# The last row tile's output in three pieces of 288, 160 and 128 columns instead of two of 288

## The chip, the cores and the metric

The kernel runs on one core of a Trainium2 chip. The time of a kernel is the device time of one execution in microseconds (us). The span of a profile is what the profiler saw of one execution; it is about 1.8 us shorter than the device time of the same run. Engines: PE is TensorE (PEld its weight loads), DVE VectorE, ACT ScalarE, SP SyncE, which here issues the stores. A semaphore is a counter that one unit raises and another waits for; a store raises its own in 16 steps, and the last step is called its landing. PSUM is the memory that matmuls write to. A drain is an instruction of an engine's queue; the first of SyncE's at the end of the program follows its waits for the stores.

## The reference

A two-layer block with squared ReLU, in bf16, on 2048 rows:

```
S, D, F = 2048, 576, 4608
h   = x @ w1 + b1            # [S, F]
h   = relu(h) ** 2
out = h @ w2 + b2            # [S, D]
```

## The kernel before

The rows are taken in four blocks of 512. For each block a first phase computes `hT` (36 tiles of 128 features), and a second one, `phase_b`, computes the output of four row tiles of 128 rows: 36 accumulated matmuls for each of two halves of 288 columns, one DVE add of the bias out of PSUM for each half, and a store. The very last row tile computes its halves one after the other, so that the first can be evacuated and stored while the second is computed:

```python
    def phase_b(sb, hT, last=False, dups=()):
        for jj in range(RT):
            ...
            po = [ps_o.tile([P, 512], FP32, name="po", tag="po") for _ in range(2)]
            o_sb = opool.tile([P, D], BF16, name="o_sb", tag="o_sb")
            # mmb(i, ft, h): matmul i of half h into po[h], 128 x 288
            # evac(h): o_sb half h = po[h] + b2_bc half h, on VectorE
            ...
            if last and jj == RT - 1:
                for h in range(2):
                    for i, ft in enumerate(ft_order):
                        mmb(i, ft, h)
                    evac(h)
                    keep(nc.sync.dma_start(out=out2[rt * P:(rt + 1) * P, h * DH:(h + 1) * DH], in_=o_sb[:, h * DH:(h + 1) * DH]))
                continue
            for i, ft in enumerate(ft_order):
                for h in range(2):
                    mmb(i, ft, h)
            for h in range(2):
                evac(h)
            keep(nc.sync.dma_start(out=out2[rt * P:(rt + 1) * P, :], in_=o_sb[:]))
```

After the kernel's last instruction, SyncE waits for the semaphores of everything still in flight; then the engines meet at two barriers and the program ends. The stores take turns on eight semaphores. The kernel's text shows none of this.

## Time and profile before

| | before |
|---|---|
| time, median of 3 runs (range) | 293.56 us (293.25 to 294.12) |
| span of the profile | 291.4 us |
| PE busy | 98% |
| last matmul starts | 287.42 us |
| last store issued, landed | 288.23, 289.80 us |

Lines from the page of the profile before: the busy time of each engine with its share of the span, then the shares of the chain that ended last.

```profile
span 291.4 us, 5457 instructions
PE 286.5 (98%) x2412; PEld 177.5 (61%) x2412; DVE 81.4 (28%) x189; ACT 93.7 (32%) x154; POOL 1.5 (1%) x8
...
PE 98%; ACT 0%; DVE 0%; issue 0%
```

PE is 98% busy and, after the loads at the start, has no idle time before its matmuls (0.0 in the groups of the page). Leaving the start aside, only two things can shorten this kernel: fewer PE cycles, or a shorter stretch after PE's last matmul. That stretch is seen in the timeline of the kernel before (start, length, engine, line, operation, count, and in brackets the idle time before it):

```profile
282.76 4.94 PE L233 MATMUL po<-w_sb,hT 128*128 128x288 bf16 x39
...
283.33 0.46 DVE L242 TENSOR_TENSOR o_sb<-po,b_bc 128x288 bf16<-128x288 f32 x1 [3.71 <-PE po L233]
283.82 4.74 SPq L254 DMA_DIRECT2D out_dram<-o_sb  x2
287.74 0.46 DVE L242 TENSOR_TENSOR o_sb<-po,b_bc 128x288 bf16<-128x288 f32 x1 [3.95 <-PE po L233]
```

The last add begins at 287.74 us and takes 0.46, and the second store follows at once. From there to the end of the span at 291.4 us there are no compute lines at all. SyncE's waits in this window (engine and line that waited, for whom, us in total, times, longest):

```profile
SPq L254 <- DVE o_sb L242: 7.7, 2, 4.0
SPq L317 <- DMA out_dram<-o_sb: 1.2, 1, 1.2
SPq L317 <- PEq L317: 0.6, 2, 0.5
```

The 1.2 us is the wait for the last store to land. L317 is the line that closes the program. The views merge what comes after it. The single records of SyncE in the trace show it (us; length in ns; the semaphores waited for):

```
288.227   332  store, increments 102
288.604    17  wait 103
288.664  1163  wait 104, 102      <- 102 lands at 289.80; the wait ends at 289.827
290.279    28  wait 106, 100      <- 452 ns after the wait before has ended
290.352    28  wait 107, 110
290.421    28  wait 108, 118
290.483    28  wait 109, 105
290.553    13  drain
```

The waits stand in a fixed order and follow each other at 60 to 73 ns when nothing blocks them. The prediction uses this order and pace in its step 4.

### The profile page before, as it was taken

The numbers are of one execution on the slowest core, as the hardware profiler recorded it, in microseconds if no ns is written. First come the engines' busy times: TensorE is split into PE (matmuls) and PEld (weight loads), VectorE is DVE, ScalarE is ACT, GpSimd is POOL, SyncE is SP. The second block draws the span as 40 slices with busy tenths as digits, with TensorE's granted clock in tenths as the row PEclk, the third lists the DMA queues.
The fourth block names the chain that finished last, engine by engine and source line by source line (L and its number), as shares of the span: only waits on it lengthen the run. The fifth ranks groups of instructions, "written<-read, shape, count | busy, mean of one in ns | idle before, by whom it ended". The sixth has DMA issues, their size and how long they took to land.

```text
span 291.4 us, 5457 instructions
## 1 busy us (share of the span) xinstructions
PE 286.5 (98%) x2412; PEld 177.5 (61%) x2412; DVE 81.4 (28%) x189; ACT 93.7 (32%) x154; POOL 1.5 (1%) x8
## 2 busy tenths in 40 slices
PE   8999999999999999999999999999999999999994
PEld 4444444444687875444477877444457878777783
DVE  3444544444531011544411110344440111110110
ACT  4666666666400001766620000466660000000000
POOL 2000000000000000000000000000000000000000
PEclk9999999999999999999999999999999999999999
DMA  6999999900000000000000000000000000000000
GB/s 183 201 200 175 233 358 326 158 7 2 0 23 0 23 20 20 2 1 2 2 0 20 23 3 20 20 2 0 2 0 2 20 24 20 23 0 23 20 23 21
DMA packets 27320, 16.05 MB, mean 55 GB/s; under 512 B 11284, under 2 KB 27296, under 8 KB 27296
## 3 DMA queue, kind: packets, MB, share of 16 engines
q1 hardware_dynamic: 26976, 15.39, 23.2%
q8 instruction: 19, 0.31, 0.4%
q10 hardware_dynamic: 288, 0.30, 0.3%
q14 instruction: 5, 0.04, 0.0%
q0 software_dynamic: 32, 0.01, 0.0%
HBM read 11.36 MB, written 2.36 MB: 47 GB/s over the span
## 4 chain that ended last, share of the span: by engine, by line
PE 98%; ACT 0%; DVE 0%; issue 0%
PE po L233 49%; PE ph L173 23%; PE ph L175 20%; PE pn L194 5%; PE wps L61 1%; PE pn L188 1%; ACT xTw L143 0%; ACT xTw L144 0%; DVE o_sb L242 0%; PE pn L190 0%; PE ta L138 0%; PE tb L141 0%; PE tb L142 0%; PE b1T_ps L151 0%
## 5 line engine op out<-in xcount | busy, mean ns | idle before, releaser
L233 PE MATMUL po<-w_sb,hT 128*128 128x288 bf16 x1152 | 141.6, 286 | 0.0
L233 PEld LDWEIGHTS <-hT 128*128 128x128 bf16 x1152 | 112.6, 98 | 29.3 <-issue 0.8
L175 PE MATMUL ph<-xTw,w_h 64*128 64x512 bf16 x576 | 125.0, 376 | 0.0
L173 PE MATMUL ph<-xTw,w_h 64*128 64x512 bf16 x576 | 125.0, 376 | 0.0
L161 ACT ACTIVATE r<-ph,b1T 128x512 bf16<-128x512 f32 x128 | 81.1, 685 | 41.0 <-PE ph L173 20.5
L162 DVE TENSOR_TENSOR hT<-r 128x512 bf16<-128x512 bf16 x144 | 61.2, 425 | 79.3 <-ACT r L161 79.3
L173 PEld LDWEIGHTS <-w_h 64*128 64x128 bf16 x576 | 54.0, 94 | 36.4
L175 PEld LDWEIGHTS <-w_h 64*128 64x128 bf16 x576 | 54.0, 94 | 32.3 <-DMA w_h<-in_w_dram 0.8
L242 DVE TENSOR_TENSOR o_sb<-po,b_bc 128x288 bf16<-128x288 f32 x32 | 13.2, 453 | 122.5 <-PE po L233 122.5
L161 ACT ACTIVATE r<-pn,b1T 128x512 bf16<-128x512 f32 x16 | 10.0, 688 | 80.9 <-PE pn L190 80.1
L194 PE MATMUL pn<-xTw,w1n 128*128 128x512 bf16 x64 | 14.5, 379 | 0.4 <-ACT xTw L144 0.4
L194 PEld LDWEIGHTS <-w1n 128*128 128x128 bf16 x64 | 6.1, 98 | 7.6 <-DMA w1n<-in_w_dram 0.6
L61 PE MATMUL wps<-const-bfloat16-1.0 128*128 128x512 bf16 (+1 forms) x7 | 2.9, 593 | 0.8 <-PEq L306 0.8
L113 DVE COPY xTw<-xTw 64x2048 bf16<-64x2048 bf16 x4 | 2.8, 688 | 0.5 <-ACT xTw L144 0.4
L114 DVE COPY xTw<-xTw 64x2048 bf16<-64x2048 bf16 x4 | 2.8, 688 | 0.1
L188 PE MATMUL pn<-xTw,w1n_89 64*128 64x512 bf16 x8 | 2.4, 380 | 0.0
L190 PE MATMUL pn<-xTw,w1n_89 64*128 64x512 bf16 x8 | 2.4, 380 | 0.0
L139 DVE COPY xTw<-ta 128x384 bf16<-128x384 bf16 x4 | 1.2, 358 | 4.1 <-PE ta L138 4.1
L61 PEld LDWEIGHTS <-const-bfloat16-1.0 128*128 128x128 bf16 x7 | 0.9, 135 | 2.1 <-issue 2.1
L98 ACT ACT_TABLE_LOAD x1 | 1.3, 1283 | 1.7 <-PEq L306 1.7
L143 ACT COPY xTw<-tb 128x128 bf16<-128x128 bf16 x4 | 1.2, 298 | 1.1 <-PE tb L142 1.1
L138 PE MATMUL ta<-ident,x_sb 128*128 128x128 bf16 x12 | 1.4, 240 | 0.0
(20 smaller groups left out, 8.4 us busy)
## 6 DMA issues: line engine op xcount, KB each, us to landing
w_sb<-in_w_dram SPq DMA_DIRECT2D x6, 864.0 KB, 11.5
w_h<-in_w_dram SPq DMA_DIRECT2D x14, 288.0 KB, 6.7
out_dram<-o_sb SPq DMA_DIRECT2D x15, 144.0 KB, 1.8
w_h<-in_w_dram SPq DMA_DIRECT2D x4, 144.0 KB, 3.4
w1n<-in_w_dram SPq DMA_DIRECT2D x4, 128.0 KB, 3.3
x_sb<-in_x_dram ACTq DMA_DIRECT2D x2, 144.0 KB, 3.1
x_sb<-in_x_dram SPq DMA_DIRECT2D x2, 144.0 KB, 2.8
b_bc<-in_b_dram SPq DMA_DIRECT2D x1, 144.0 KB, 6.1
```

The costliest lines, as they stand in the source:

```text
L61: keep(nc.tensor.matmul(wps[:, 0:n], lhsT=ones[:, 0:P], rhs=ones[:, 0:n], start=True, stop=True))
L113: keep(nc.vector.tensor_copy(out=xT[0:H, SPC:SPC + 4, :], in_=xT[H:P, E3:E3 + 4, :]))
L114: keep(nc.vector.tensor_copy(out=xT[H:P, SPC:SPC + 4, :], in_=xT[0:H, O:O + 4, :]))
L161: keep(nc.scalar.activation(out=r[:], in_=bank[:], func=ACT.Relu, bias=b1T[:, ft:ft + 1], scale=1.0))
L162: keep(nc.vector.tensor_tensor(out=hTs[sb][:, ft, :], in0=r[:], in1=r[:], op=ALU.mult))
L173: keep(nc.tensor.matmul(bx[:], lhsT=w1_h[0:H, LO_C[i], jc], rhs=xT[0:H, LO_W[i], :], start=(i == 0), stop=(i == NC - 1)))
L175: keep(nc.tensor.matmul(by[:], lhsT=w1_h[H:P, UP_C[i], jc], rhs=xT[H:P, UP_W[i], :], start=(i == 0), stop=(i == NC - 1)))
L188: keep(nc.tensor.matmul(banks[2 * i][:], lhsT=w1n8[0:H, i, :], rhs=xT[0:H, SPC, :], start=start, stop=stop))
L190: keep(nc.tensor.matmul(banks[2 * i + 1][:], lhsT=w1n8[H:P, i, :], rhs=xT[H:P, E3, :], start=start, stop=stop))
L194: keep(nc.tensor.matmul(banks[g][:], lhsT=w1n[:, k, g * P:(g + 1) * P], rhs=xT[:, O + k, :], start=start, stop=stop))
L233: keep(nc.tensor.matmul(po[h][:, 0:DH], lhsT=hT[:, ft, jj * P:(jj + 1) * P], rhs=w2_sb[:, ft, h * DH:(h + 1) * DH], start=(i == 0), stop=( ...
L242: keep(nc.vector.tensor_tensor(out=o_sb[:, h * DH:(h + 1) * DH], in0=po[h][:, 0:DH], in1=b2_bc[:, h * DH:(h + 1) * DH], op=ALU.add,))
```

## The change

Its intent is to shorten the exposed tail: when PE finishes, only 128 columns are left to add and to store instead of 288. The price is a third group of 36 matmuls, with 36 more weight loads, and a third store.

```diff
             if last and jj == RT - 1:
-                for h in range(2):
+                edges = [0, DH, D - P, D]
+                for n in range(3):
+                    d0, d1 = edges[n], edges[n + 1]
+                    pl = ps_o.tile([P, 512], FP32, name="po", tag="po") if n == 2 else po[n]
                     for i, ft in enumerate(ft_order):
-                        mmb(i, ft, h)
-                    evac(h)
-                    keep(nc.sync.dma_start(out=out2[rt * P:(rt + 1) * P, h * DH:(h + 1) * DH], in_=o_sb[:, h * DH:(h + 1) * DH]))
+                        keep(nc.tensor.matmul(pl[:, 0:d1 - d0], lhsT=hT[:, ft, jj * P:(jj + 1) * P],
+                                              rhs=w2_sb[:, ft, d0:d1], start=(i == 0), stop=(i == NFT - 1)))
+                    keep(nc.vector.tensor_tensor(out=o_sb[:, d0:d1], in0=pl[:, 0:d1 - d0],
+                                                 in1=b2_bc[:, d0:d1], op=ALU.add))
+                    keep(nc.sync.dma_start(out=out2[rt * P:(rt + 1) * P, d0:d1], in_=o_sb[:, d0:d1]))
                 continue
```

## The prediction

> What bounds the kernel now. The page of the profile gives PE busy 98% of a span of 291.4 us at a granted clock of 0.999; the chain of waits is 98% PE. The change touches only the last row tile. In the timeline its 72 matmuls of 288 columns start 122.5 ns apart (the last at 287.42 us), so they are array-bound; the weight loads, 98 ns each, are hidden. The Trainium skill ("TensorE: Matmul & The Clock Gate", "Back-to-back issue gap") gives N/2.4 + 2.5 ns = 122.5; the trace agrees. After PE comes an exposed tail of 3.9 us: 0.32 us from the start of the last matmul to the DVE add, the add of 128x288 (0.458), 0.03 to the issue of the store, 1.58 until it lands (289.80), then some 1.5 us of end-of-program waits and barriers. Only this tail can shrink.
>
> What the change does.
> 1. PE: 36 matmuls of 288 columns become 36 of 160 and 36 of 128. The columns stay, so only the fixed part per matmul is added, if the 36 more weight loads stay hidden. By the same formula 69.2 and 55.8 ns: 36 x (69.2 + 55.8 - 122.5) = +0.09 us. The trace supports it: the 128-column transposes at 4.0 to 4.8 us start 55.7 ns apart, each with its own 128x128 weight load shown as 98 ns, so weight loads overlap each other. The same section states 81 ns as the sustained spacing for N = 128; if that held for both pieces, PE would lose 36 x (2 x 81 - 122.5) = 1.4 us. I think it unlikely: PE's sequencer runs ahead of the array (its drain is recorded 2.4 us, some 19 matmuls, before the end), and that lead feeds most of 72 short matmuls.
> 2. DVE: the last add shrinks from 288 to 128 columns. Estimated from the trace's adds and multiplies (about 158 ns fixed plus 1.04 ns a column from PSUM): 0.29 us, so -0.17 us.
> 3. Store: the last piece is 32 KB instead of 72. The 144 KB stores take 1.8 us to landing, the 72 KB ones 1.6 to 2.1, so size matters little; the data moves in 0.36 us (8 packets of 576 B per engine, 28 ns each; 1152 B take 50). 256 B packets: perhaps -0.1 us, nothing if small writes carry a fixed cost. The 160-column store is issued about 2 us earlier, so it is landing when the last is issued; no queueing.
> 4. End of program: SyncE waits for the store semaphores one after another, 60 to 70 ns each. One more store moves the last one to the next semaphore in turn, which is waited for first: about +0.06 us.
> 5. PSUM: the third piece takes the buffer of an output evacuated some 8 us before; no wait.
>
> All of it is on the critical path and nearly cancels: +0.09 - 0.17 - 0.1 + 0.06 = -0.12 us, 0.04% of the time, below the spread of the runs before (293.25 to 294.12).
>
> Predicted: 293.45 us, 8 in 10 within 293.0 to 294.0. Faster by over 2%: 0.005; within 2%: 0.99; slower by over 2%: 0.005.
>
> What would show each step: matmul starts 69 and 56 ns apart in the last two pieces; the last DVE add near 0.29 us; the last store landing 1.5 to 1.6 us after issue; the stretch from the tile's first matmul to the last add longer by 0.1 us.
>
> What would make it wrong: weight loads or instruction supply pacing the short matmuls at 80 to 98 ns (+1.4 to +2.5 us, still within 2%); the third store queueing behind the second; 256 B writes landing later.

## The result

| | before | changed |
|---|---|---|
| time, median (range) | 293.64 us (293.25 to 294.32), 6 runs | 293.02 us (292.90 to 293.61), 6 runs |
| ratio | | 0.998, 95% interval 0.9965 to 0.9996 |
| span of the profile | 291.4 us | 291.2 us |

Here and below a ratio is the mean time of one kernel's fast runs over that of the other's of the same rounds, so it is not quite the ratio of the medians. The changed kernel is within 2% of the one before, about 0.6 us faster, and its interval lies just under 1.

The timeline of the changed kernel at its end, in the same columns:

```profile
282.81 5.40 PE L255 MATMUL po<-w_sb,hT 128*128 128x288 bf16 x78
...
283.74 0.46 DVE L257 TENSOR_TENSOR o_sb<-po,b_bc 128x288 bf16<-128x288 f32 x1 [3.71 <-PE po L255]
284.23 4.67 SPq L259 DMA_DIRECT2D out_dram<-o_sb  x3
286.23 0.33 DVE L257 TENSOR_TENSOR o_sb<-po,b_bc 128x160 bf16<-128x160 f32 x1 [2.03 <-PE po L255]
288.24 0.29 DVE L257 TENSOR_TENSOR o_sb<-po,b_bc 128x128 bf16<-128x128 f32 x1 [1.69 <-PE po L255]
```

The last add is 0.29 us, as predicted. It starts later on the clock of this profile than before (288.24 against 287.74), although the work before it is the same but for 0.09 us. The reason is at the other end of the trace: in this execution PE waited longer for weights during the loads. The groups of the two pages have it, the kernel before first, then the changed one (idle time before the group, and its releaser, at the end of the line).

```profile
L175 PE MATMUL ph<-xTw,w_h 64*128 64x512 bf16 x576 | 125.0, 376 | 0.0
```

```profile
L175 PE MATMUL ph<-xTw,w_h 64*128 64x512 bf16 x576 | 125.0, 376 | 0.4 <-DMA w_h<-in_w_dram 0.4
```

So the span compares two loading phases as well as two tails. Over the 13 profiles in which the tile before the last is untouched, its first add starts anywhere from 278.79 to 279.88 us. I therefore measure the tail from that add to the end of the span. The links of the tail, read from the single records (us):

| link | before | changed | difference | predicted |
|---|---|---|---|---|
| first add of the tile before the last -> start of the last matmul | 8.619 | 8.776 | +0.157 | |
| -> start of the last add | 0.323 | 0.257 | -0.066 | +0.09 with the line above |
| the last add | 0.458 | 0.291 | -0.167 | -0.17 |
| -> issue of the last store | 0.028 | 0.028 | 0.000 | 0 |
| -> its landing (16th increment of its semaphore) | 1.577 | 1.459 | -0.118 | -0.1 |
| -> the drain that ends SyncE's waits | 0.749 | 0.401 | **-0.348** | **+0.06** |
| -> end of the span | 0.817 | 0.814 | -0.003 | 0 |
| tail | 12.571 | 12.026 | -0.545 | -0.12 |

Every term but one is as predicted. PE lost 0.157 - 0.066 = 0.09 us. The starts of the short matmuls are 69 and 56 ns apart. The groups of the changed kernel between 283 and 289 us, with shapes kept apart (count; busy us and mean ns of one; idle before) show both sorts of matmul beside the weight loads. First the groups of the kernel before, between 283.2 and 289 us:

```profile
L233 PE MATMUL po<-w_sb,hT 128*128 128x288 bf16 x37 | 4.7, 286 | 0.0
L233 PEld LDWEIGHTS <-hT 128*128 128x128 bf16 x35 | 3.4, 98 | 0.9
```

```profile
L255 PEld LDWEIGHTS <-hT 128*128 128x128 bf16 x76 | 5.0, 98 | 0.1
L255 PE MATMUL po<-w_sb,hT 128*128 128x160 bf16 x36 | 2.7, 233 | 0.0
L255 PE MATMUL po<-w_sb,hT 128*128 128x128 bf16 x36 | 2.2, 219 | 0.0
```

A weight load is still recorded at 98 ns, yet PE has no idle time and 36 matmuls of 160 and of 128 columns take 2.7 and 2.2 us. These are busy times, which include the modelled end of the last matmul; start to start they are 2.49 and 2.01.

The unexpected gain is in the end waits, which were to cost 0.06 us and gave back 0.35. SyncE's waits in the same window:

```profile
SPq L266 <- DVE o_sb L242: 8.4, 1, 8.4
SPq L259 <- DVE o_sb L257: 7.3, 3, 3.8
SPq L322 <- DMA out_dram<-o_sb: 1.1, 1, 1.1
SPq L322 <- PEq L322: 0.6, 2, 0.5
```

The last two lines are as before, but for 0.1 us. The view of waits can't see the difference, because the 0.45 us gap is no wait for anybody. The single records of SyncE in the changed kernel do:

```
288.563   332  store, increments 103   <- lands at 290.022
290.038    17  wait 103
290.101    28  wait 104, 102
290.170    28  wait 106, 100
290.232    28  wait 107, 110
290.296    28  wait 108, 118
290.358    28  wait 109, 105
290.423    13  drain
```

One wait more stands behind the landing, as predicted, but the pause is gone. Nearly two thirds of the gain in the trace (0.348 of 0.545 us) would thus not come from the smaller last piece at all. What made the pause go?

### The profile page after: what moved, and what is told of

Same layout as the page of the kernel before. It is cut to its first block, busy times and chain, and to the rows that moved or that the text cites. A ratio compares the mean times of both kernels' runs of the same rounds, so it can differ in the third digit from the quotient of the medians.

```text
span 291.2 us, 5529 instructions
## 1 busy us (share of the span) xinstructions
PE 286.3 (98%) x2445; PEld 178.6 (61%) x2448; DVE 81.5 (28%) x190; ACT 93.5 (32%) x154; POOL 1.5 (1%) x8
## 4 chain that ended last, share of the span: by engine, by line
PE 94%; DMA 3%; SPq 2%; issue 0%; DVE 0%
PE po L233 45%; PE ph L173 21%; PE ph L175 20%; PE pn L194 4%; PE po L255 3%; DMA w_h<-in_w_dram 2%; SPq L80 1%; DMA x_sb<-in_x_dram 1%; SPq L77 0%; PE pn L188 0%; PE pn L190 0%; DVE o_sb L257 0%
## 5 line engine op out<-in xcount | busy, mean ns | idle before, releaser
L233 PE MATMUL po<-w_sb,hT 128*128 128x288 bf16 x1080 | 132.8, 286 | 0.0
L242 DVE TENSOR_TENSOR o_sb<-po,b_bc 128x288 bf16<-128x288 f32 x30 | 12.3, 453 | 114.8 <-PE po L233 114.8
L255 PE MATMUL po<-w_sb,hT 128*128 128x288 bf16 (+2 forms) x108 | 9.1, 246 | 0.0
L257 DVE TENSOR_TENSOR o_sb<-po,b_bc 128x288 bf16<-128x288 f32 (+2 forms) x3 | 1.1, 358 | 7.4 <-PE po L255 7.4
```

The source lines that it names most:

```text
L233: keep(nc.tensor.matmul(po[h][:, 0:DH], lhsT=hT[:, ft, jj * P:(jj + 1) * P], rhs=w2_sb[:, ft, h * DH:(h + 1) * DH], start=(i == 0), stop=( ...
L242: keep(nc.vector.tensor_tensor(out=o_sb[:, h * DH:(h + 1) * DH], in0=po[h][:, 0:DH], in1=b2_bc[:, h * DH:(h + 1) * DH], op=ALU.add,))
L255: keep(nc.tensor.matmul(pl[:, 0:d1 - d0], lhsT=hT[:, ft, jj * P:(jj + 1) * P], rhs=w2_sb[:, ft, d0:d1], start=(i == 0), stop=(i == NFT - 1)))
```

## The experiments

The first theory (A): the pause belongs to the way of waiting, since before, SyncE was blocked on the second of two semaphores in one wait, and in the changed kernel on a wait with one semaphore. An extra store moves the last one to the next semaphore. Its rival (B): the end waits got shorter because the last piece is smaller.

"Tail" and "landing to last drain" in what follows are links of the table above ("last drain" is the drain that ends SyncE's waits). All results of all runs were correct.

### Extra store, last tile untouched

The store of one earlier row tile is cut in two; the last store moves from semaphore 102 to 103.

```diff
+            if (sb, jj) in [(2, 0)]:
+                for h in range(2):
+                    keep(nc.sync.dma_start(out=out2[..., h * DH:(h + 1) * DH], in_=o_sb[:, h * DH:(h + 1) * DH]))
+                continue
             keep(nc.sync.dma_start(out=out2[rt * P:(rt + 1) * P, :], in_=o_sb[:]))
```

> The kernel before with the store of one earlier row tile cut in two halves; the last tile is untouched. The last store then gets the semaphore that SyncE waits for first at the end, as in the changed kernel. Theory A (the gain is mostly the end-of-program wait: a wait blocked on the second of two semaphores is followed by 0.45 us of nothing): from the landing of the last store to SyncE's last drain 0.40 us instead of 0.75, from the start of the first add of the tile before the last to the end of the span about 12.2 us instead of 12.57, time 0.35 us (0.12%) below before: 293.3. Theory B (the gain belongs to the smaller last piece): 12.57 us and no change, 293.6.

Measured: landing to last drain 0.407 us, tail 12.29 us. The gain in the end waits is there without any change to the last tile, so theory B falls. The time does not show it: 293.86 us (5 runs, 293.08 to 294.27) against 293.70, ratio 1.0001 (0.9988 to 1.0014). The profiled run's last-but-one tile came 0.9 us later than in the profile before, from the loading phase; 0.28 us of tail is lost in such scatter. Five rounds do not resolve this, the trace does.

### The change with two stores

Three pieces of compute, the first two stored by one DMA; the last store is back on semaphore 102.

```diff
-                    keep(nc.sync.dma_start(out=out2[..., d0:d1], in_=o_sb[:, d0:d1]))
+                    s0 = 0 if n == 1 else d0
+                    if n > 0:
+                        keep(nc.sync.dma_start(out=out2[..., s0:d1], in_=o_sb[:, s0:d1]))
```

> The changed kernel with its three pieces of compute, but the first two pieces stored by one DMA, so that the last store is on the semaphore of before again. Theory A: the 0.45 us pause after the wait comes back, landing to last drain 0.75 us, tail from the add of the tile before about 12.38 us, time 0.19 us below before (0.07%). Theory B: tail 12.03 us, 0.55 us below before.

Measured: landing to last drain 0.747 us, with 0.44 us of pause in the same place as before; tail 12.39 us. The small last piece alone is worth 0.18 us. Time 293.50 us, ratio 0.9998 (0.9984 to 1.0012).

### Two pieces, 448 and 128 columns

```diff
-                edges = [0, DH, D - P, D]
-                for n in range(3):
+                edges = [0, D - P, D]
+                for n in range(2):
```

> Two pieces, 448 and 128 columns: no added matmul, the last add and store as small as in the change, last store on the semaphore of before. Both theories: PE gains 0.00 instead of +0.09, add -0.17, store -0.12. Theory A: the pause stays, tail 12.57 - 0.28 = 12.29 us, time 0.28 us below before (0.1%). Theory B: tail about 11.94 us, 0.63 us below.

Measured: tail 12.30 us, landing to last drain 0.762 us (pause 0.46). The start of the last matmul is 8.686 us after the reference add, and the add 0.257 us after that: 8.943 us in all, against 8.942 before. So a two-piece split with a small last piece has the gain of the three-piece one at no cost to PE. Time 293.45 us, ratio 0.9989 (0.9977 to 1.0002).

### The same with six earlier stores cut in two

The edit is that of the two runs "448 and 128" and "extra store", with six tiles in the list.

> As the run with 448 and 128, with six earlier row-tile stores cut in halves, so that the last store is on the semaphore that SyncE waits for last. Theory A: the other five waits are done before the landing, so after it only one wait and the drain remain: landing to last drain about 0.1 us (0.55 if a two-semaphore wait pauses wherever it is blocked), tail about 11.65 us (12.1), time about 0.9 us (0.45) below before. Theory B: the order doesn't matter; same time as the run with 448 and 128.

Measured: landing to last drain 0.084 us, tail 11.61 us, time 292.71 us (292.58 to 292.78, 5 runs) against 293.70, ratio 0.9964 (0.9952 to 0.9977). The order of the waits is a cost of its own: five of the six waits are now done while the store is on its way. With the last store on 102 and no pause, 0.308 us lie there (the run with eight extra stores, below); here it is 0.084.

Up to here theory A fits every number. But it had been fitted to one pause, and all these runs changed two things at once: which semaphore is blocked, and how many instructions SyncE has.

### The change with one and with six extra stores

> The changed kernel with one earlier store cut in two, so that its last store moves on to the semaphore that stands first in SyncE's second, two-semaphore wait (before, the second place of the same wait was blocked). If the pause comes only after a wait blocked in its second place: no pause, landing to last drain 0.34 us (0.40 less one wait). If it belongs to that wait instruction whichever of its semaphores blocks: about 0.75 us.

Measured: 0.331 us, no pause in the end waits: the same wait, blocked in its first place.

> The changed kernel with six earlier stores cut in two, so that its last store is on the semaphore that stands second in SyncE's third wait. If a block in the second place pauses in any wait: landing to last drain 0.68 us (0.75 less one wait). If the pause belongs to the second wait alone: 0.27 us.

Measured: 0.247 us, no pause in the end waits, although this wait was blocked for 0.98 us in its second place. The general form of theory A fails here. What remained was "that wait, blocked on 102" (called A' below), which explains nothing, or a new theory C: the pause is at a fixed place in SyncE's instruction stream, whatever it waits for. SyncE has 88 recorded instructions in the three kernels that paused in the end waits and 90 or more in all others; each extra store adds two, the store and a wait before its semaphore is used again.

### Stream length and semaphore taken apart

Three looks separate them. An earlier store issued from ScalarE's queue shortens SyncE's stream by two and leaves the turn of the semaphores as it is:

```diff
-            keep(nc.sync.dma_start(out=out2[rt * P:(rt + 1) * P, :], in_=o_sb[:]))
+            eng = nc.scalar if (sb, jj) in [(2, 0)] else nc.sync
+            keep(eng.dma_start(out=out2[rt * P:(rt + 1) * P, :], in_=o_sb[:]))
```

> The kernel before with one earlier row tile stored from ScalarE's queue instead of SyncE's; nothing else moves, the last store stays on the same semaphore, but SyncE's instruction stream is two instructions shorter (86 recorded instead of 88). Theory A' (the 0.45 us pause belongs to a block in the second place of SyncE's second end wait): the pause stays where it is, 0.45 us right after that wait, landing to last drain 0.75 us. Theory C (the pause is SyncE getting its next instructions, at a fixed place of its stream): it moves two instructions later, or vanishes.

> The kernel before with eight earlier stores cut in two: the semaphores have gone once round, so the last store is on the same semaphore as before, with SyncE's stream 16 instructions longer (104). Theory A': pause of 0.45 us after the second end wait, landing to last drain 0.75 us. Theory C: no pause there, 0.33 us.

> The changed kernel with one earlier row tile stored from ScalarE's queue: the last store stays on the semaphore waited for first, but SyncE's stream is as long as that of before (88). Theory A': no pause, landing to last drain 0.40 us. Theory C: a pause of about 0.45 us between SyncE's second and third end wait, as in before, though another semaphore was blocked: landing to last drain 0.80 us.

Measured, with SyncE's records at the end of the three runs (start in us, length in ns):

```
before, one store from ScalarE (86)    before + 8 stores (104)      changed, one store from ScalarE (88)
288.845    17  wait 103                289.470    17  wait 103      289.614    17  wait 103  (blocked)
288.909  1142  wait 104, 102           289.528  1162  wait 104,102  289.674    28  wait 104, 102
290.094    28  wait 106, 100           290.725    28  wait 106,100  290.146    28  wait 106, 100   <- 444 ns
290.164    28  wait 107, 110           290.789    28  wait 107,110  290.225    28  wait 107, 110
290.636    28  wait 108, 118 <- 444 ns 290.851    28  wait 108,118  290.294    28  wait 108, 118
290.715    28  wait 109, 105           290.910    28  wait 109,105  290.356    28  wait 109, 105
```

| run | recorded SyncE instructions | last store on | pause | landing to last drain |
|---|---|---|---|---|
| before | 88 | 102 | 452 ns after wait 2 | 0.749 us |
| before, one store from ScalarE | 86 | 102 | 444 ns after wait 4 | 0.756 us |
| before, eight extra stores | 104 | 102 | none in the end waits | 0.308 us |
| changed | 90 | 103 | none to be seen | 0.401 us |
| changed, one store from ScalarE | 88 | 103 | 444 ns after wait 2 | 0.827 us |

Theory C predicted all three, and A' was wrong in all three. With two instructions fewer the pause moves by two instructions. With the same semaphore and a longer stream it is gone from the end waits. With the changed kernel's semaphore and the old length it is back. In each case it stands after the 79th recorded instruction of SyncE. The traces of the longer streams have it at that place too, where it does no harm: in the changed kernel with one extra store SyncE does nothing for 447 ns between its 79th record, the second-last store, and its 80th, at 288.03 us. In the runs with six and eight extra stores and in the one with 128-column pieces below, the same 447 to 452 ns lie between the 79th and the 80th at 245 to 266 us. That is 12 of 14 traces. In the other two, the changed kernel and the one with an extra store before, the 80th is the wait for the last store, so a pause there passes unseen while the store is on its way. A second sign says that it is there: in the 12 an instruction transfer of 8 KB starts 0.61 to 0.68 us after the start of the 80th record. In the other two such a transfer starts at 289.97 and 290.55 us, 0.63 and 0.62 us after the moment at which a pause of 447 ns would have ended. One point of the expectation was off: for the second run I expected 0.33 us and the trace has 0.31.

Why SyncE stops there is not settled. That it fetches more instructions at that point is the obvious reading. The Trainium skill ("Runtime: NRT & Kernel Launch", "Instruction fetch mechanics") describes a sequencer that fetches its instructions in blocks through a DMA queue of its own, and calls the cost of crossing a block "mostly hidden". The pause is tied to a place in the stream, which agrees with blocks, and 0.44 us is not hidden. But the 8 KB instruction transfer that goes with it starts after the pause (at 290.9 us in the trace before), so no record shows a fetch that SyncE waited for. As every run was profiled, it is not shown either that an execution without the profiler has the pause.

### A long stream of short matmuls

The prediction rested on short matmuls not being held up by weight loads or by the supply of instructions, and gave as the reason that PE's sequencer (the part that hands it its instructions) runs ahead of the array. Here all four row tiles of the last phase are cut into 128, 128, 128, 128 and 64 columns.

```diff
-            if last and jj == RT - 1:
-                edges = [0, DH, D - P, D]
-                for n in range(3):
+            if last:
+                edges = [0, P, 2 * P, 3 * P, 4 * P, D]
+                for n in range(5):
```

> All four row tiles of the last phase in pieces of 128, 128, 128, 128 and 64 columns: 144 matmuls of 128 columns in a row, eight times what the sequencer's lead of some 20 matmuls can feed. If the array sets the pace (as in the change): starts 55.8 ns apart throughout; last phase 4 x 36 x (4 x 55.8 + x) us, with x 29 ns at 64 columns if weight loads stay hidden, more if a weight load has a floor. If instructions or weight loads pace a long stream: 81 ns (as the skill page states as sustained) once the lead is used up, some 10 us longer in all.

Measured: starts 55.8 ns apart at 128 columns and 29.1 at 64, throughout. Time 294.26 us (one run). When PE's sequencer reached its drain, 17 matmuls were still to start; it is 17 before and in the changed kernel too. So the lead was not used up: it is the same after 720 short matmuls, the last 36 of them 29 ns apart. The groups of this run between 253 and 292 us, and the busy time of two stretches of it, one of 128-column matmuls and one of 64 (stretch; length; then PE, PEld, DVE, ACT and POOL busy with counts, clock, DMA share, GB/s):

```profile
L255 PEld LDWEIGHTS <-hT 128*128 128x128 bf16 x720 | 36.5, 98 | 0.1
L255 PE MATMUL po<-w_sb,hT 128*128 128x128 bf16 x576 | 32.8, 219 | 0.0
L255 PE MATMUL po<-w_sb,hT 128*128 128x64 bf16 x144 | 4.9, 193 | 0.0
```

```profile
255.00:259.00 4.00, 4.00 (x75) 4.00 (x73) 0.58 (x2) 0.00 (x0) 0.00 (x0) 1.00 0.17 52
261.00:262.00 1.00, 1.00 (x34) 1.00 (x32) 0.29 (x1) 0.00 (x0) 0.00 (x0) 1.00 0.06 16
```

PEld reads as fully busy in both, at 75 matmuls in 4 us and at 34 in 1 us. A weight load recorded at 98 ns overlaps the next ones; its length says nothing of the pace it allows. The skill page ("TensorE: Matmul & The Clock Gate", "Back-to-back issue gap") gives N/2.4 + 2.5 ns for a matmul by itself, and 81 ns as the sustained spacing in a stream of weight loads and matmuls at N = 128. The first form fits at every size (122.5, 69.2, 55.8, 29.1 ns at 288, 160, 128, 64 columns), the second doesn't hold here.

### Smaller last pieces

Both with six extra stores, so that the order of the waits is best and no pause falls into them.

> Pieces of 512 and 64 columns with the last store on the semaphore waited for last. If weight loads stay hidden at 64 columns (29.2 ns a matmul): tail about 11.5 us, 0.1 us better than with 448 and 128 (11.61). If a weight load can't follow faster than about 56 ns, PE loses 36 x 27 ns = 0.96 us and the tail is about 12.45 us, slower than with 448 and 128.

Measured: the matmuls are as fast as hoped (8.711 us to the last start), but the last store took 1.64 us to landing, against 1.41 for a store of the same size in the run before this one. Its issue took 0.56 us instead of 0.33: it came 0.58 us after the issue of a store of 128 KB. Tail 11.73 us, 0.2 us more than expected. Time 292.65 us (292.01 to 293.46, 6 runs) against 293.68, ratio 0.9965 (0.9948 to 0.9981).

> Pieces of 480 and 96 columns, six earlier stores cut in two (last store on the semaphore waited for last, no pause in SyncE's end waits): the compromise between 448 + 128 (tail 11.61 us) and 512 + 64 (11.73, its last store landing 0.2 us late behind the large one before it). By the terms measured so far: last matmul start 8.70 us after the first add of the tile before, 0.24 to the add, add 0.26, 0.03, store 1.43, one wait 0.08, end 0.82: tail 11.56 us, time 0.95 to 1.05 us below before (292.7). If the large store delays the last one here too: 11.7 us.

Measured: last store issued in the usual 0.33 us and landed in 1.449, tail 11.58 us, as expected. Its groups from 279 to 290 us show that the larger first add, 0.66 us, is over long before the last one; the last piece's add is down to 0.26:

```profile
L257 DVE TENSOR_TENSOR o_sb<-po,b_bc 128x480 bf16<-128x480 f32 x1 | 0.7, 657 | 6.6 <-PE po L255 6.6
...
L257 DVE TENSOR_TENSOR o_sb<-po,b_bc 128x96 bf16<-128x96 f32 x1 | 0.3, 258 | 0.9 <-PE po L255 0.9
```

Time 292.44 us (292.20 to 293.09, 5 runs) against 293.60, ratio 0.997 (0.9956 to 0.9983). The three two-piece versions with six extra stores are 0.9 to 1.1 us faster than the kernel before by the ratios (0.9964 x 293.70 = 292.6; 0.997 x 293.60 = 292.7). Among themselves they can't be told apart by time; by the tail, 480 and 96 is the shortest. Against the changed kernel (tail 12.03 us) it is 0.45 us shorter in the trace.

## Why the prediction was right, and where it was not

The measured 293.02 us lies in the range of 293.0 to 294.0, by 0.02 us, and "within 2%" came true. That was partly luck: the forecast gain was 0.12 us and the measured one 0.6, and the range, about as wide as the scatter of the runs before, let it pass. Step by step:

1. **PE, +0.09 us.** Right: +0.157 to the start of the last matmul, -0.066 from there to the add. The reason given for it was only half right. That the sequencer's lead "feeds most of 72 short matmuls" was not needed: the lead is still 17 matmuls at the end of 720 short ones.
2. **DVE, -0.17 us.** Right, -0.167.
3. **Store, -0.1 us.** Right, -0.118. A packet of 256 B takes 17.6 ns where one of 576 B takes 28.5, and the packets of the last store span 0.26 us instead of 0.36. The store before it did not delay it: its last packet ended at 287.70 us, before the issue at 288.56.
4. **End of program, "about +0.06 us".** Wrong in sign: -0.348. The step as put, that the last store moves to "the next semaphore in turn, which is waited for first", was right and costs +0.09 (0.308 us without the pause on 102, against 0.401 on 103). What it left out is the 0.44 us pause, which lay open in the trace before and which the third store's two instructions pushed to a place where it does no harm: 0.093 - 0.441 = -0.348.
5. **PSUM.** Right: no wait before the third piece.

The sum of the trace is -0.545 us instead of -0.12. The ratio of 0.998 makes it -0.6 us, with an interval of -0.1 to -1.0. The cause shown by the traces, mostly one of each kernel, is thus: 0.2 us from the smaller last piece (-0.167 - 0.118 + 0.09), which is the intent of the change, and 0.35 us from where SyncE's instruction stream happens to end. The second part came with an extra store in the kernel before too, with nothing else changed. The time could not have shown this, as the loading phase moves the whole kernel by up to a microsecond from one profile to the next.

## What to carry to other kernels

When a change is worth less than the scatter of the start, measure from a late event that it does not touch to the end, and take that stretch apart link by link. In an exposed tail, count every record after the last compute, and ask of every gap what it is before predicting: here two instructions more or fewer in SyncE's queue moved a pause in or out of it, which looked like the effect of whatever was changed. An uneven split in two (480 and 96 here) gave a small last piece and the shortest tail in the traces, at no cost to PE. With 512 and 64 the store before was so large and so late that the last one took 0.2 us longer (size and lateness were not tested apart).

## What the Trainium skill lacked or had wrong

- "Runtime: NRT & Kernel Launch", "Instruction fetch mechanics": it calls the cost of crossing a block of instructions mostly hidden. Here SyncE stops for 0.44 to 0.46 us after its 79th recorded instruction in the 12 traces of 14 in which it can be seen. In five of them that place came to lie behind the last store's wait, and the whole pause was exposed. (That the pause is a fetch is inferred.)
- No page has the cost of the waits that end a program: 60 to 73 ns for each wait of SyncE that stands behind the last landing (0.40 us with six of them, 0.08 with one), so the semaphore on which the last store falls is worth up to 0.3 us.
- "TensorE: Matmul & The Clock Gate", "Back-to-back issue gap": 81 ns is given as the sustained spacing at N = 128 with weight loads. Measured: 55.8 ns over 576 matmuls, each with its own load.
- The same page, "LDWEIGHTS (loading the stationary operand)": P / 1.2 gives an estimate of 107 ns for 128 columns. The trace has 98 ns each, and loads start as little as 29 ns apart without slowing the matmuls.
- "Trainium Kernel Development and Optimization", "Best Practices": it recommends the busy share of LDWEIGHTS, beside MFU, as a measure of the distance to the roofline. Here the profile's busy share of PEld, which counts overlapping loads once, reads 100% at 55.8 ns a matmul and at 29.1 ns alike.
- "DMA: Bandwidth & Descriptors", "Specifications": below 512 B a transfer is said to need a read-modify-write. The lengths of the stores' packets in the traces show no step there: 12.6, 14.7, 17.6, 19.7, 28.5 and about 50 ns for packets of 128, 192, 256, 320, 576 and 1152 B. From the last packet's end to the landing it is 0.38 us at 576 B (before) and 0.36 at 256 B (changed).
